# Modulation vectors by transposed loads and dot products, V in a tile of its own, two sets of gate and up weights

## The chip, the cores and the metric

One core of one Trainium2 chip runs the whole kernel. The metric is the device time of one execution in microseconds (us). Before the change the median of 10 runs is 1286.09 us (1285.23 to 1288.04).

## The reference

A transformer block on 2048 tokens of width 1024, in bfloat16, whose two layer norms are modulated by a conditioning vector c:

```python
mod = (_silu(c) @ w_mod).reshape(1, 6, 1, -1)      # c: 1 x 1024, w_mod: 1024 x 6144
sa, ca, ga, sb, cb, gb = (mod[:, i] for i in range(6))
h = layernorm(x) * (1 + ca) + sa
x = x + ga * attention(h)
h = layernorm(x) * (1 + cb) + sb
x = x + gb * ((silu(h @ w_gate) * (h @ w_up)) @ w_down)
```

The attention has 32 query heads of 128 columns over 4 cached key and value heads, of which the last 512 positions are used: q = h @ wq, scores scaled by 128 ** -0.5, softmax, times V, then the output projection wo (4096 x 1024). The inner width of the feed-forward part (FFN) is 3584. All weights are bfloat16.

## The kernel before

A guarded fast path (`fast_path`) does all the work; a general path follows only if a bound computed on the side says that the softmax without a maximum might overflow.

The tokens are cut into four chunks `cc` of 512. The attention is one sequence of 128 head units `k` (4 chunks x 32 heads). In unit `k` the program emits the scores of head `k` (`emit_s`, L1032: four matmuls of 512 columns, and two exponentials on ScalarE, L1034, which give `pT`), the q projection of head `k + 3` (`emit_q`, L1019: eight matmuls; VectorE casts the result to `qT`, L916), the side tasks planned for that unit, and the product with V of head `k - 1` (`emit_o`, L1064: 4 token tiles x 4 value blocks `j`, with `pT` as weights and V as the moving operand). A column of ones beside V makes the same matmul give the softmax denominator; VectorE takes its reciprocal (L1046) and scales (L1051) when three token tiles have filled a PSUM bank. The token tiles of one head come in groups of three that run on over heads.

Side tasks are written down by hand with `at(k, ...)`: the output projection (`emit_wo`, L1096, eight matmuls a unit from unit 13 on, evicted by VectorE at L1102, L1104 or L1108 to L1111), layer-norm statistics and transposes for later chunks, loads of x and wo, and a sum of squares of wq (`bound_wq`, L955) from unit 32 on. The modulation vectors are among them. Shift and scale of the first norm (`sa`, `ca1`) are made at the start (`mod_cols`, L753). The other four come in two rounds of 16 units: `load_rows` loads w_mod in natural layout, 1 MB at a time; `mod_rows` (L779) multiplies it with `sil32` (silu(c) repeated over 32 columns), four matmuls side by side in column groups of 32; VectorE evicts (L784, L788) into a block called `row`; the result goes to DRAM (`row_d`), and is read back as a broadcast row (`load_gate`, for the gates `ga_bc` and `gb_bc`) or as columns (`load_cols`, for `cb1` and `sb`; `cb1` gets one added on VectorE, L802).

After unit 127 comes the FFN, chunk by chunk: seven groups `fg` of four inner tiles, each with four weight tiles of 512 KB (two of w_gate, two of w_up; `load_gu`, `emit_gu` L1168), then the down projection (`emit_down`, L1188) in two halves `dh` of 512 output columns, each with seven w_down tiles (`load_wd`). The last output-projection units run between the first FFN groups.

In SBUF, blocks of some 4 KB per partition are shared by pools: `blkA` (8 buffers: `pT`, accumulators, the FFN's products), `blkB` (7: kT, V, wq, then gate and up weights) and `blkC` (13: `oq`, `oT`, `wo`, `row`, then w_down). w_mod pieces and normalized chunks share the pool `hT` (4). PSUM has a pool `mm` of 4 banks for q, o, output projection and down projection, and a pool `s` of 2 double banks for scores and the FFN.

While the attention is emitted, all loads and DMA transposes go through SP's queue (`fetch`, L664; `xpose_o`, L1081; `ln_xpose`, L848) in program order, and the vector instructions marked with `pin` keep their order. In the FFN the framework's scheduler orders the loads. A buffer that is still in use holds up the load that is to fill it, and with it the queue. Outputs leave by ScalarE's queue.

Of the kernel before, what the change touches and what calls it, by code (L numbers as in the profile page):

```python
# [9 lines left out]
ALU = mybir.AluOpType  # L10
AX = mybir.AxisListType
BF16 = mybir.dt.bfloat16
# [576 lines left out]
def fast_path(ctx, tc, flag, A_x, A_k_cache, A_v_cache, A_wq, A_wo, B_x, B_w_gate, B_w_up,  # L589
# [3 lines left out]
    nc = tc.nc  # L593
# [37 lines left out]
    hpool = ctx.enter_context(tc.tile_pool(name="hT", bufs=4))  # L631
    pa_ = ctx.enter_context(tc.tile_pool(name="blkA", bufs=8))
    pb_ = ctx.enter_context(tc.tile_pool(name="blkB", bufs=7))
    pc_ = ctx.enter_context(tc.tile_pool(name="blkC", bufs=13))
    wk = ctx.enter_context(tc.tile_pool(name="work", bufs=2))
    sm = ctx.enter_context(tc.tile_pool(name="small", bufs=4))
    psp = ctx.enter_context(tc.tile_pool(name="psum", bufs=4, space=bass.MemoryType.PSUM))
# [5 lines left out]
    def blkB(name, shape, dt=BF16):  # L643
        return pb_.tile(shape, dt, name=name, tag="B")
# [57 lines left out]
    for kv in range(Hkv):  # L702
        pin(nc.sync.dma_start_transpose(
            out=kT[:, kv, :], in_=A_k_cache[0, kv, k0:k0 + W, :]), "dma")
    VW = Dh + 4
    v_sb = blkB("v_sb", [P, Hkv, WT, VW])
    for kv in range(Hkv):
        load(v_sb[:, kv, :, 0:Dh], v_v[:, kv])
    nc.gpsimd.memset(v_sb[:, :, :, Dh:VW], 1.0)
    load_wq(0, 1)  # L710


# [45 lines left out]

    sil32 = const.tile([P, DT, 32], BF16, name="sil32")
    for dt in range(DT):
        nc.vector.tensor_scalar(out=sil32[:, dt, :], in0=ones_bf[:, 0:32],
                                scalar1=siluc[:, dt:dt + 1], scalar2=None, op0=ALU.mult)
    wm_rows = []
    row_part = []
    row_d = {}

    def load_rows(vec, part):
        t = hpool.tile([P, 4, D], BF16, name="wmr", tag="hT")  # L770
        load(t, wm_v[:, 4 * part:4 * part + 4, vec * D:(vec + 1) * D])
        wm_rows.append(t)

    def mod_rows(n, part):
        ps = mm("row_ps")
        tiles = [wm_rows.pop(0) for _ in range(2)]
        for k in range(4):
            for i in range(4):
                nc.tensor.matmul(ps[32 * i:32 * i + 32, :], lhsT=sil32[:, 4 * part + k, :],  # L779
                                 rhs=tiles[i // 2][:, k, (i % 2) * 512:(i % 2 + 1) * 512],  # L780
                                 start=(k == 0), stop=(k == 3))
        if part == 0:
            r = blkC("row", [P, TCW], FP32)
            nc.vector.tensor_copy(out=r, in_=ps)  # L784
            row_part.append(r)
        else:
            r = row_part.pop()
            nc.vector.tensor_tensor(out=r, in0=ps, in1=r, op=ALU.add)  # L788
            d = dp.tile([4, TCW], FP32, name="row_d", tag="row_d", bufs=2)
            fetch(out=d, in_=r[0:P:32, :])  # L790
            row_d[n] = d

    def load_gate(n, k, dst):
        fetch(out=dst.rearrange("p (a b) -> p a b", a=2),
                          in_=row_d[n][k:k + 2, :].partition_broadcast(P))

    def load_cols(n, k, dst, add_one):
        src = row_d[n][k:k + 2, :].rearrange("a (b p) -> p (a b)", p=P)
        with nc.allow_non_contiguous_dma(reason="1024 values to columns"):
            fetch(out=dst, in_=src)  # L800
        if add_one:
            nc.vector.tensor_scalar(out=dst, in0=dst, scalar1=1.0, scalar2=None, op0=ALU.add)  # L802

    tasks = {}

# [248 lines left out]
    def emit_o(g):  # L1054
        cc, h = divmod(g, H)
        kv = h // rep
        if h % 4 == 0:
            oq[(cc, h // 4)] = blkC("oq", [P, QT, 4, Dh])
        for t in range(QT):
            if o_slot["n"] == 0:  # L1060
                o_slot["ps"] = mm("o_ps", (P, SLOTS, Dh + 1))
            s_ = o_slot["n"]
            for j in range(WT):
                nc.tensor.matmul(o_slot["ps"][:, s_, :], lhsT=pT[g][:, j, t * P:(t + 1) * P],  # L1064
                                 rhs=v_sb[:, kv, j, 0:Dh + 1], start=(j == 0),
                                 stop=(j == WT - 1))
            runs = o_slot["runs"]
            if runs and runs[-1][0] == g:
                runs[-1][2] = t + 1
            else:  # L1070
                runs.append([g, t, t + 1, s_])
            o_slot["n"] = s_ + 1
            if o_slot["n"] == SLOTS or (t == QT - 1 and h % HQ == HQ - 1):
                close_bank()
        del pT[g]
# [35 lines left out]
            nc.vector.tensor_tensor(out=x1, in0=f, in1=x1, op=ALU.add)  # L1111


    for n, vecs in enumerate(((2, 4), (5, 3))):
        for part in range(2):
            k = 16 * n + 8 * part
            at(k, load_rows, vecs[0], part)
            at(k + 2, load_rows, vecs[1], part)
            at(k + 5, mod_rows, n, part)
        at(16 * n + 15, load_gate, n, 0, gb_bc if n else ga_bc)  # L1120
        at(16 * n + 16, load_cols, n, 2, sb if n else cb1, n == 0)
    for tt in range(QT, S // P):
        cc, t = divmod(tt, QT)
        at(max((cc - 1) * H - 16, 0) + 2 + 2 * t, load_x, tt)
# [26 lines left out]
    gu_w = {}  # L1151
    wd_tiles = {}

    def load_gu(cc, fg):
        for nm, v in (("wg", wg_v), ("wu", wu_v)):
            for i in range(2):
                t = blkB(nm, [P, 4, 512])
                load(t, v[:, 4 * i:4 * i + 4, fg * 512:(fg + 1) * 512])
                gu_w[(cc, fg, nm, i)] = t

# [113 lines left out]
```

## Time and profile before

| | |
|---|---|
| median of 10 runs | 1286.09 us |
| lowest, highest | 1285.23, 1288.04 us |
| the profiled execution: its time | 1285.31 us |
| its span, first to last instruction | 1283.5 us |
| TensorE's granted clock, mean | 0.998 |
| TensorE busy (matmuls) | 1263.0 us, 98% |
| VectorE busy | 578.1 us, 45% |
| ScalarE busy | 334.0 us, 26% |
| DMA | 204.20 MB, 159 GB/s on average |
| q, scores, o matmuls | 1024 and 512 of 512 columns, 2048 of 129 columns |
| row matmuls for four modulation vectors | 64 of 512 columns, 32 weight columns each |

The profile is of one execution. The page gives busy time, instruction groups by line, and waits; the trace behind it can be asked for a stretch of time, a line or a tile. Matmuls are pipelined, so the recorded length of one is longer than the distance to the next: distances between starts tell what a matmul costs. A few per cent of matmul records are missing. Units of the attention last 3.5 us up to unit 12 (without an output projection) and 5.24 us from unit 14 on.

### The profile page before, as it was taken

What the parts mean: (1) busy time and instruction counts of PE and PEld (TensorE: products, weight loads), DVE (VectorE), ACT (ScalarE), POOL (GpSimd) and SP (SyncE); (2) the same over time, 40 slices, a digit from 0 to 9 for tenths busy, and PEclk for the clock granted to TensorE, in tenths of its full rate; (3) what the DMA queues carried; (4) which work ended last, traced back from release to release, by engine and by line L of the source; (5) the groups of instructions that cost most, each with busy time, mean ns of one, the idle gap of its engine ahead of it and who ended that gap; (6) DMA issues with size and microseconds to landing.
All of it is one profiled execution on the core that took longest, in us unless ns stands there. A gap on an engine that the chain in (4) does not pass through costs nothing.

```text
span 1283.5 us, 18000 instructions
## 1 busy us (share of the span) xinstructions
PE 1263.0 (98%) x7461; PEld 644.1 (50%) x7601; DVE 578.1 (45%) x1271; ACT 334.0 (26%) x433; POOL 1.3 (0%) x8
## 2 busy tenths in 40 slices
PE   8999999999999999999999999999999999999998
PEld 4555555555555555555554444444444444444444
DVE  4464567866577755576663642221212121221122
ACT  3543334343333433333341111011100111011100
POOL 0000000000000000000000000000000000000000
PEclk9999999999999999999999999999999999999999
DMA  9878466456345654445568384454536445454401
GB/s 290 275 203 220 162 149 172 135 144 202 96 123 156 148 140 148 116 148 131 132 171 272 124 251 151 140 188 144 179 104 219 142 163 165 135 193 133 146 19 34
DMA packets 280107, 204.20 MB, mean 159 GB/s; under 512 B 113865, under 2 KB 273609, under 8 KB 280018
## 3 DMA queue, kind: packets, MB, share of 16 engines
q1 hardware_dynamic: 275106, 198.78, 52.3%
q10 hardware_dynamic: 4912, 4.20, 1.0%
q8 instruction: 61, 1.00, 0.3%
q14 instruction: 28, 0.23, 0.1%
HBM read 174.08 MB, written 4.21 MB: 139 GB/s over the span
## 4 chain that ended last, share of the span: by engine, by line
PE 96%; DMA 2%; DVE 1%; issue 1%; SPq 0%; ACT 0%; DVEq 0%
PE gu_ps L1168 29%; PE a_ps L1096 17%; PE q_ps L1019 17%; PE d_ps L1188 15%; PE o_ps L1064 9%; PE s_ps L1032 8%; DMA wm<-in_w_mod_dram 1%; PE q_ps L940 0%; DMA modT<-row_d 0%; DMA wu<-in_B_w_up_dram 0%; PE row_ps L779 0%; DMA hT<-xn 0%; SPq L664 0%; PE mod_ps L753 0%; DVE st L816 0%
## 5 line engine op out<-in xcount | busy, mean ns | idle before, releaser
L1034 ACT ACTIVATE pT<-s_ps 128x1024 bf16<-128x1024 f32 x256 | 248.6, 1020 | 343.8 <-PE s_ps L1032 229.6
L1096 PE MATMUL a_ps<-wo,oT 128*128 128x512 bf16 x986 | 239.9, 379 | 3.0 <-DVE acc L1102 1.0
L1019 PE MATMUL q_ps<-hT,wq 128*128 128x512 bf16 x999 | 236.7, 379 | 0.3 <-DVE modT L755 0.3
L1168 PE MATMUL gu_ps<-hT,wu 128*128 128x512 bf16 x875 | 209.9, 379 | 1.8 <-DMA wu<-in_B_w_up_dram 0.7
L1168 PE MATMUL gu_ps<-hT,wg 128*128 128x512 bf16 x879 | 210.0, 379 | 0.9
L1174 DVE TENSOR_TENSOR guT<-gu_ps,sg 128x512 bf16<-128x512 f32 x112 | 77.4, 691 | 283.7 <-ACT sg L1173 283.7
L1173 ACT ACTIVATE sg<-gu_ps 128x512 bf16<-128x512 f32 x112 | 66.9, 597 | 489.6 <-PE gu_ps L1168 426.9
L1188 PE MATMUL d_ps<-wd,guT 128*128 128x512 bf16 (+2 forms) x935 | 193.3, 366 | 0.9
L916 DVE CAST qT<-q_ps 128x512 bf16<-128x512 f32 x128 | 88.3, 691 | 177.2 <-PE q_ps L1019 176.7
L1096 PEld LDWEIGHTS <-oT 128*128 128x128 bf16 x1024 | 99.9, 98 | 122.3 <-issue 2.1
L1019 PEld LDWEIGHTS <-wq 128*128 128x128 bf16 x1000 | 97.8, 98 | 117.8 <-issue 0.3
L1064 PEld LDWEIGHTS <-pT 128*128 128x128 bf16 x2048 | 128.4, 97 | 30.6 <-issue 0.4
L1188 PEld LDWEIGHTS <-guT 128*128 128x128 bf16 x952 | 90.9, 98 | 103.0
L1168 PEld LDWEIGHTS <-wu 128*128 128x128 bf16 x896 | 87.6, 98 | 106.7 <-DMA wu<-in_B_w_up_dram 1.2
L1168 PEld LDWEIGHTS <-wg 128*128 128x128 bf16 x896 | 87.7, 98 | 105.5
L1064 PE MATMUL o_ps<-v_sb,pT 128*128 128x129 bf16 x2048 | 139.2, 219 | 0.0
L1032 PE MATMUL s_ps<-qT,kT 128*128 128x512 bf16 x467 | 128.9, 378 | 3.0 <-ACT pT L1034 0.6
L1051 DVE TENSOR_TENSOR oq<-o_ps,rl 128x256 bf16<-128x256 f32 (+2 forms) x256 | 101.3, 420 | 4.3
L1192 DVE TENSOR_TENSOR f<-d_ps,gb_bc 128x512 f32<-128x512 f32 (+2 forms) x34 | 22.5, 660 | 147.0 <-PE d_ps L1188 133.2
L1104 DVE TENSOR_TENSOR acc<-a_ps,acc 128x512 f32<-128x512 f32 x64 | 44.1, 689 | 40.8 <-PE a_ps L1096 40.8
L1032 PEld LDWEIGHTS <-kT 128*128 128x128 bf16 x512 | 44.7, 97 | 31.9 <-issue 1.3
L816 DVE BATCH_NORM_STATS2 st<-x 128x6 f32<-128x512 bf16 x64 | 41.3, 680 | 2.6 <-DMA x<-in_A_x_dram 2.4
(75 smaller groups left out, 307.6 us busy)
## 6 DMA issues: line engine op xcount, KB each, us to landing
wq<-in_A_wq_dram SPq DMA_DIRECT2D x64, 512.0 KB, 4.3
wo<-in_A_wo_dram SPq DMA_DIRECT2D x64, 512.0 KB, 5.4
wg<-in_B_w_gate_dram SPq DMA_DIRECT2D x56, 512.0 KB, 4.8
wu<-in_B_w_up_dram SPq DMA_DIRECT2D x56, 512.0 KB, 5.5
wd<-in_B_w_down_dram SPq DMA_DIRECT2D x56, 512.0 KB, 7.1
wmr<-in_w_mod_dram SPq DMA_DIRECT2D x8, 1024.0 KB, 8.7
x<-in_A_x_dram SPq DMA_DIRECT2D x16, 256.0 KB, 5.4
wm<-in_w_mod_dram SPq DMA_DIRECT2D x4, 1024.0 KB, 10.4
```

The source lines that it names most:

```text
L916: nc.vector.tensor_copy(out=t, in_=q_ps)
L1019: nc.tensor.matmul(q_ps, lhsT=wq_tiles[(cc, h // 4, dt // 4)][:, dt % 4, (h % 4) * P:(h % 4 + 1) * P], rhs=hT[("h1", cc)][:, dt, :], start ...
L1032: nc.tensor.matmul(s_ps[:, i, :], lhsT=kT[:, kv, j * P:(j + 1) * P], rhs=qT[g], start=True, stop=True)
L1034: nc.scalar.activation(out=p[:, 2 * jj:2 * jj + 2, :], in_=s_ps, func=ACT.Exp, scale=scale)
L1051: nc.vector.tensor_tensor(out=dst, in0=ps[:, s0:s0 + cnt, 0:Dh], in1=sc, op=ALU.mult)
L1064: nc.tensor.matmul(o_slot["ps"][:, s_, :], lhsT=pT[g][:, j, t * P:(t + 1) * P], rhs=v_sb[:, kv, j, 0:Dh + 1], start=(j == 0), stop=(j == W ...
L1096: nc.tensor.matmul(a_ps, lhsT=oT[(cc, 2 * q + i)][:, hh % 4, t * P:(t + 1) * P], rhs=wo_tiles[(cc, q, dh, i)][:, hh % 4, :], start=(hh == ...
L1104: nc.vector.tensor_tensor(out=acc[(cc, t)][:, dsl], in0=a_ps, in1=acc[(cc, t)][:, dsl], op=ALU.add)
L1168: nc.tensor.matmul(ps[:, n, :], lhsT=gu_w[(cc, fg, nm, dt // 4)][:, dt % 4, fi * P:(fi + 1) * P], rhs=hT[("h2", cc)][:, dt, :], start=(dt ...
L1173: nc.scalar.activation(out=g, in_=ps[:, 0, :], func=ACT.Silu)
L1174: nc.vector.tensor_tensor(out=guT[(cc, fg)][:, fi, :], in0=ps[:, 1, :], in1=g, op=ALU.mult)
L1188: nc.tensor.matmul(d_ps, lhsT=guT[(cc, f // 4)][:, f % 4, t * P:(t + 1) * P], rhs=wd_tiles[(cc, dh, f // 4)][:, f % 4, c0:c0 + w], start=( ...
```

## The change

Four things change together.

V moves out of `blkB` into a tile of its own, with 160 elements (320 bytes) per row instead of 132 (264 bytes), two ones columns instead of four, and 130 columns in the o matmul instead of 129. So `blkB` has six buffers for wq during the attention instead of five.

The four later modulation vectors are no longer made on TensorE. silu(c) goes to DRAM as a row and comes back broadcast over the partitions (`c_bc`). w_mod is loaded by DMA transposes, four of [1024 x 128] for each half vector, one half vector every four units from unit 1 to 29. In each of the units 4 to 35 VectorE does one dot product of 1024 elements per partition, which gives 128 values of a modulation vector as one column. `cb1` and `sb` are then in place (one is added to `cb1`); the two gates go to DRAM as columns and come back as broadcast rows. `sil32`, `row` and the row matmuls are gone.

`blkC` has 12 buffers instead of 13.

In the FFN the fourth tile of every second group (the second half of w_up) is loaded into the first 4096 bytes of V's tile, which by then is free. With the seven buffers of `blkB` that makes eight tiles, two full sets.

```diff
-    pc_ = ctx.enter_context(tc.tile_pool(name="blkC", bufs=13))
+    pc_ = ctx.enter_context(tc.tile_pool(name="blkC", bufs=12))
...
-    VW = Dh + 4
-    v_sb = blkB("v_sb", [P, Hkv, WT, VW])
+    VN = Dh + 2
+    v_sb = const.tile([P, Hkv, WT, Dh + 32], BF16, name="v_sb")
...
-    nc.gpsimd.memset(v_sb[:, :, :, Dh:VW], 1.0)
+    nc.gpsimd.memset(v_sb[:, :, :, Dh:VN], 1.0)
...
-    def load_rows(vec, part):
...
-    def mod_rows(n, part):
...
-    def load_cols(n, k, dst, add_one):
...
+    def spread_c():
+        fetch(out=c_d, in_=sil_r)
+        fetch(out=c_bc.rearrange("p (a b) -> p a b", a=DT), in_=c_d.partition_broadcast(P))
+
+    def load_wmT(vec, part):
+        t = hpool.tile([P, 4, D], BF16, name="wmT", tag="hT")
+        for i in range(4):
+            c0 = vec * D + (4 * part + i) * P
+            pin(nc.sync.dma_start_transpose(out=t[:, i, :], in_=w_mod[:, c0:c0 + P]), "dma")
+        wm_cols[(vec, part)] = t
+
+    def mod_dot(vec, j, dst):
+        t = wm_cols[(vec, j // 4)]
+        junk = wk.tile([P, D], BF16, name="junk", tag="junk", bufs=1)
+        pin(nc.vector.scalar_tensor_tensor(out=junk, in0=t[:, j % 4, :], scalar=1.0, in1=c_bc,
+                                           op0=ALU.mult, op1=ALU.mult,
+                                           accum_out=dst[:, j:j + 1]))
+
+    def add_one(dst):
+        pin(nc.vector.tensor_scalar(out=dst, in0=dst, scalar1=1.0, scalar2=None, op0=ALU.add))
+
+    def store_gate(n):
+        d = dp.tile([DT, P], FP32, name="col_d", tag="col_d", bufs=2)
+        with nc.allow_non_contiguous_dma(reason="columns to 1024 values"):
+            fetch(out=d.rearrange("a p -> p a"), in_=mod_col[:, n, :])
+        col_d[n] = d
+
+    def load_gate(n, dst):
+        fetch(out=dst.rearrange("p (a b) -> p a b", a=DT), in_=col_d[n].partition_broadcast(P))
...
-                o_slot["ps"] = mm("o_ps", (P, SLOTS, Dh + 1))
+                o_slot["ps"] = mm("o_ps", (P, SLOTS, VN))
...
-                                 rhs=v_sb[:, kv, j, 0:Dh + 1], start=(j == 0),
+                                 rhs=v_sb[:, kv, j, 0:VN], start=(j == 0),
...
-    for n, vecs in enumerate(((2, 4), (5, 3))):
+    at(0, spread_c)
+    for i, (vec, dst) in enumerate(((2, mod_col[:, 0, :]), (4, cb1), (3, sb),
+                                    (5, mod_col[:, 1, :]))):
         for part in range(2):
-            k = 16 * n + 8 * part
-            at(k, load_rows, vecs[0], part)
-            at(k + 2, load_rows, vecs[1], part)
-            at(k + 5, mod_rows, n, part)
-        at(16 * n + 15, load_gate, n, 0, gb_bc if n else ga_bc)
-        at(16 * n + 16, load_cols, n, 2, sb if n else cb1, n == 0)
+            k = 1 + 8 * i + 4 * part
+            at(k, load_wmT, vec, part)
+            for j in range(4):
+                at(k + 3 + j, mod_dot, vec, 4 * part + j, dst)
+        k = 1 + 8 * i + 10
+        if vec == 4:
+            at(k, add_one, cb1)
+        elif vec in (2, 5):
+            at(k + 1, store_gate, vec // 5)
+            at(k + 2, load_gate, vec // 5, gb_bc if vec == 5 else ga_bc)
...
+    v_flat = v_sb.rearrange("p a b c -> p (a b c)")
+    v_blk = v_flat[:, 0:2048].rearrange("p (a b) -> p a b", a=4)
...
-                t = blkB(nm, [P, 4, 512])
+                spare = (cc * NFG + fg) % 2 == 1 and nm == "wu" and i == 1
+                t = v_blk if spare else blkB(nm, [P, 4, 512])
```

More of the change, by code (lines that the diff above doesn't have):

```diff
@@ L756, in mod_cols @@
                                 scalar1=1.0 if add_one else 0.0, scalar2=None, op0=ALU.add)
[L761 to L767, printed above, removed]
-    def load_rows(vec, part):
-        t = hpool.tile([P, 4, D], BF16, name="wmr", tag="hT")
-        load(t, wm_v[:, 4 * part:4 * part + 4, vec * D:(vec + 1) * D])
-        wm_rows.append(t)
@@ L774, in mod_rows @@
-    def mod_rows(n, part):
[L775 to L791, printed above, removed]
@@ L793, in load_gate @@
-    def load_gate(n, k, dst):
-        fetch(out=dst.rearrange("p (a b) -> p a b", a=2),
-                          in_=row_d[n][k:k + 2, :].partition_broadcast(P))
-    def load_cols(n, k, dst, add_one):
[L798 to L802, printed above, removed]
+    c_d = dp.tile([DT, P], BF16, name="c_d", tag="c_d", bufs=1)
@@ new lines, in fast_path @@
+    c_bc = const.tile([P, D], BF16, name="c_bc")
+    mod_col = const.tile([P, 2, DT], FP32, name="mod_col")
+    wm_cols = {}
+    col_d = {}
+    def spread_c():
[7 more added lines that the diff above has]
+        wm_cols[(vec, part)] = t
```

## The prediction

> **What bounds the kernel now.** I read the page's first part, then the list of what TensorE waited for, then TensorE's instructions in order of time, and last the vector and DMA-issuing queues around the few places where TensorE pauses.
>
> ```profile
> PE 1263.0 (98%) x7461; PEld 644.1 (50%) x7601; DVE 578.1 (45%) x1271; ACT 334.0 (26%) x433; POOL 1.3 (0%) x8
> ```
>
> TensorE is the bound nearly everywhere, so only its own time and its pauses count. Its waits are few (columns: total us, times, longest):
>
> ```profile
> PE mod_ps L753 <- DMA wm<-in_w_mod_dram: 2.0, 2, 1.2
> PE a_ps L1096 <- DVE acc L1102: 1.0, 1, 1.0
> PE gu_ps L1168 <- DMA wu<-in_B_w_up_dram: 0.7, 1, 0.7
> ```
>
> The timeline of TensorE from 42 us on (start, length, instruction) shows the row matmuls between the q and o matmuls of one head:
>
> ```profile
> 43.45 1.89 PE L1019 MATMUL q_ps<-hT,wq 128*128 128x512 bf16 x8
> 45.27 1.05 PE L779 MATMUL row_ps<-wmr,sil 128*32 128x512 bf16 x16
> 46.25 1.10 PE L1064 MATMUL o_ps<-v_sb,pT 128*128 128x129 bf16 x16
> 47.19 1.02 PE L1032 MATMUL s_ps<-qT,kT 128*128 128x512 bf16 x3
> ```
>
> Starts are what matter, since lengths overlap. In dense stretches a 512-column matmul starts every 215.8 ns (eight in 1.726 us), so q ended at 43.45 + 1.73 = 45.17, yet o began at 46.25: the 16 row matmuls cost 1.08 us. The vector queue at 86 to 92 us shows the pause of L1096:
>
> ```profile
> 86.74 0.54 DVE L835 TENSOR_SCALAR xn<-x,mv 128x1024 bf16<-128x1024 bf16 x1
> 90.94 0.17 DVE L802 TENSOR_SCALAR modT<-modT 128x8 f32<-128x8 f32 x1 [3.66 <-DMA modT<-row_d]
> 91.02 0.69 DVE L816 BATCH_NORM_STATS2 st<-x 128x6 f32<-128x512 bf16 x1
> 91.62 0.68 DVE L1102 COPY acc<-a_ps 128x512 f32<-128x512 f32 x1
> ```
>
> The add-one on cb1 holds VectorE 3.66 us for a DMA; the accumulator copy behind it frees its PSUM bank late. Start to start, TensorE loses 1.18 us there. Near 754.5 us, a late half of w_up costs 0.87 us, also by starts. From 29 us to the last matmul I find no other pause of 30 ns or more besides the four row groups.
>
> **What the Trainium skill says.** "TensorE: Matmul & The Clock Gate", "Wait, 56ns, not 53.3ns?", spaces warm matmuls by N/2.4 ns + about 2.5: 215.8 for 512 agrees. For 129 it gives 56.25, but the o groups disagree: averaged over the trace by position, starts after value block j=0, 1, 2, 3 are 56.1, 59.9, 55.8, 59.4 ns apart, mean 57.8. "SBUF — State Buffer", "Specifications (TRN2)", names 16-byte lines with a penalty for crossings. V rows of 264 bytes start at 0 or 8 within such a line in turn, which fits the alternation; so would an odd column count. The change removes both. The opening table of the TensorE page makes VectorE's queue strictly first in, first out: L802 above agrees. "DMA: Bandwidth & Descriptors", "Latency and other measured facts", gives 261 GB/s for a transpose with a non-contiguous middle dimension; here the 256-byte packets of transposes take 17 ns each on 16 engines, 241 GB/s.
>
> **The change, part by part.** Sums are against the profiled execution: span 1283.45, its own time 1285.31, against a median of 1286.09.
>
> *Row matmuls.* Four groups disappear: 1.08 + 1.06 + 1.07 + 1.08 = 4.29 us saved on TensorE.
>
> *The column fetch.* cb1 no longer comes through a DMA that VectorE waits for: 1.18 us saved. Its add-one now follows a dot product on the same queue.
>
> *V.* 130 columns give 130/2.4 + 2.5 = 56.7 ns by the page; the even blocks' 55.83 plus 0.42 gives 56.25. I take 56.4. Saved: 2048 x (57.8 - 56.4) = 2.9 us. Bounds: 3.2 us if 56.25 holds; if neither alignment nor parity matters, a loss of 2048 x 0.42 = 0.9.
>
> *Gate and up buffers.* Eight tiles (seven of blkB and the first 4096 bytes of V) let a set load during the whole set before it. Only one TensorE wait is there to remove: 0.87; I count it whole (bounds 0 and 0.9). During attention the freed slot does nothing: wq has at most four tiles live at its loads.
>
> *blkC 13 to 12.* By allocation and last use I count at most four oT, six wo and two oq live, 12; row, the thirteenth, is gone. In the FFN dh=1 then has five w_down tiles ahead instead of six; the sixth starts when dh=0's last block (6.04 us) passes its first four matmuls and is used some 9 us later, against 7.1 us to landing. Without that cover each of the four switches from dh=0 to dh=1 would wait up to a landing, 7 us. I count 0.
>
> *Vector work.* 32 dot products of 1024 elements. The nearest row is L955, 1.216 us plus 0.083 for its accumulator read: 32 x 1.30 = 41.6 us, one per head in units 4 to 35. Removed: 8 scalings (1.2), four row evictions (2.8), and the wait. The rest of the queue is what it must fit beside. VectorE by stretch (heads 10-12, 13-17, 32-35, 36-44; columns: from and to, length, VectorE busy, its instructions, granted clock, DMA share, GB/s):
>
> ```profile
> 61.20:71.80 10.60, 6.47 (x19) 1.00 0.84 152
> 71.80:100.20 28.40, 16.98 (x41) 1.00 0.87 245
> 175.70:196.70 21.00, 14.63 (x34) 1.00 0.51 130
> 196.70:243.90 47.20, 38.16 (x85) 1.00 0.60 168
> ```
>
> The first becomes 6.47 + 3.9 = 10.4 of 10.6; the second 16.98 - 0.7 + 6.5 = 22.8 of 26.1; the third 14.6 + 5.2 = 19.8 of 21. The fourth runs at 81% today without a pause. Behind a dot product wait the qT cast, the acc copy and the bank evictions, and for those TensorE's four PSUM banks; L802 showed that 4.4 us of lateness cost 1.2, so some 3 us are covered. Heads 10-12 with their statistics build up about 2 us. I charge 1.5 us (bounds 0 and 10).
>
> *DMA queue.* Eight 1 MB loads (0.5 us of issue each) become 32 transposes of 256 KB; both move 8 MB. At 17 ns per 256-byte packet that is 1.09 us of all engines each, 34.8 in all, where 2 KB packets of 88 ns took 22.5. Issue time per transpose:
>
> ```profile
> L1081 SPq DMA_TRANSPOSE oT<-oq x128: 1188/1256/3296, 43.4 to 680.8; - x128
> L703 SPq DMA_TRANSPOSE kT<-in_A_k_cache_dram x4: 1266/1486/2937, 14.8 to 20.9; - x4
> ```
>
> (minimum/median/maximum ns.) At 1.25 that is 40 us of SP's queue, in fours at heads 1, 5, 9 and so on, ahead of each next wq load. Also c_bc must wait on SP until c_d has landed: the like pair gd_d, gd_row took 3 us in a quiet queue, and here two weight loads stand before it, so c_bc goes out near 31 us, four transposes fill 31.5 to 36.6, and the wq halves for head 8 go out at 36.7 and 38 instead of 26.5 and 30, wanted at 43.4 and 44.3, with 4.3 us to landing. Later, oT leaves SP at most 2 us late, and head 16's second wq half goes out about 64.7, wanted near 71.3. Margins of 1 to 2.5 us; I charge 0.9 (bounds 0 and 15). The gate stores (1024 four-byte pieces each) have a head before their reader; the before's fetch of such pieces landed in 5.1 us. Start-up isn't touched: VectorE's 1.2 us of scalings lie beside TensorE's wait for wm.
>
> *Sum.* Saved 4.29 + 1.18 + 2.9 + 0.87 = 9.2; new pauses 2.4; net -6.8. Profiled 1285.31 - 6.8 = 1278.5; a median stood 0.78 above it, so **1279.3 us**.
>
> **Rivals.**
> *VectorE becomes the bound.* Heads 10-13 and 32-35 have no room left, and if each of their eight dot products comes through to TensorE, 10.4 us are lost, net +1.2: 1287.3, no measurable change. For it: 98% in heads 10-12. Against it: 81% sustained costs nothing now. 13%.
> *Transposes hold up SP, and the change is slower.* w_mod's rows lie 12 KB apart, and no transpose here reads such a source. Twelve are issued before head 16's wq; each us over 1.25 delays that load 12 us, less 2.6 of margin. It decides where 12d - 2.6 outgrows about 7.7 (9.2 less VectorE's 1.5), at d = 0.86, 2.1 us apiece; at 2.5 us the pause is 12.4, net +4.7: 1290.8. For it: kT's first took 2.9[...], and engines are at 0.77 to 0.87 here. Against: wm reads 1 KB pieces of the same rows at the rate of contiguous wq. 15%.
> *V's padding and the buffers do nothing.* o stays at 57.8 and the w_up wait stays: 1279.3 + 2.9 + 0.9 = 1283.1, just at the bound. 10%, half of it no change.
>
> **How the numbers follow.** The forecast holds with 62%, from 1276.9 (no new pause) to 1282. About 0.2% (2.6 us) is what a measurement can tell from no change. Faster: 62 + 5 and 1 from a mild VectorE case, 68%; same: 5 + 11, 16%; slower: 15 and 1, 16%. From 1276.5 to 1288 leaves out 3% below and some 15% above.
>
> **What would show it.** Right: no L779 rows; o groups of 16 start to next start 0.90 us instead of 0.925; no DVE wait for modT; no w_up wait; 32 accumulating VectorE instructions of 1.2 us. Wrong: TensorE waits on qT, acc or pT at heads 10-17 or 32-40 (VectorE); TensorE waits on wq, or transposes of 2 us and more at 31 to 75 us (SP); VectorE waiting for wmT or c_bc; w_down waits after 800 us (blkC).

## The result, and the profile after

The changed kernel takes 1295.19 us in the median (1293.66 to 1300.01, 9 runs); the kernel before, beside it, 1286.21 (1284.76 to 1290.16, 30 runs). The ratio is 1.007, with a 95% interval of 1.006 to 1.008: slower by about 9 us, where 7 us faster was forecast. The profiled execution took 1294.26 us, with a span of 1292.5, against 1285.31 and 1283.5 before.

The page's first part, changed kernel: TensorE has 65 fewer instructions and is busy 2 us less, and yet the span is 9 us longer. The time is in pauses.

```profile
PE 1260.9 (98%) x7396; PEld 641.2 (50%) x7537; DVE 607.3 (47%) x1323; ACT 333.9 (26%) x433; POOL 1.2 (0%) x8
```

TensorE's waits in the changed kernel (us in total, times, longest us). The two waits that the change was to remove, for `acc` behind `modT` and for w_up, are gone. A wait for the q weights stands in their place, and a small one for `guT`, the FFN's product from VectorE, near the spot where w_up used to be late:

```profile
PE q_ps L1014 <- DMA wq<-in_A_wq_dram: 11.8, 3, 6.0
PE mod_ps L753 <- DMA wm<-in_w_mod_dram: 0.9, 1, 0.9
PE gu_ps L1174 <- DVE guT L1180: 0.7, 1, 0.7
```

TensorE's timeline near 44 us, where the row matmuls stood (start, length, instruction). The q matmuls are followed at once by o, and o to s_ps is 0.90 us, as forecast for groups of 16 (it was 0.94):

```profile
44.43 1.89 PE L1014 MATMUL q_ps<-hT,wq 128*128 128x512 bf16 x8
46.16 1.07 PE L1059 MATMUL o_ps<-v_sb,pT 128*128 128x130 bf16 x16
47.06 1.03 PE L1027 MATMUL s_ps<-qT,kT 128*128 128x512 bf16 x3
```

VectorE's timeline at 86 to 92 us: where it sat 3.66 us for `modT`, it now takes a dot product (1.22 us plus 0.08 for reading the accumulator), and the `acc` copy follows without a gap:

```profile
87.69 1.22 DVE L783 SCALAR_TENSOR_TENSOR junk<-wmT,c_bc 128x1024 bf16<-128x1024 bf16 x1
88.83 0.08 DVE L783 DVE_READ_ACCUMULATOR junk<-wmT,c_bc 128x1 f32 x1
88.83 0.55 DVE L830 TENSOR_SCALAR xn<-x,mv 128x1024 bf16<-128x1024 bf16 x1
89.28 0.69 DVE L1097 COPY acc<-a_ps 128x512 f32<-128x512 f32 x1
```

VectorE over the stretches of the forecast (from and to, length, VectorE busy, its instructions, granted clock, DMA share, GB/s). Later stretches hold slightly earlier heads than before, since up to 12 us have been lost by then. None is full; the first is at 90%:

```profile
61.20:71.80 10.60, 9.59 (x24) 1.00 1.13 209
71.80:100.20 28.40, 19.63 (x46) 1.00 0.78 146
196.70:243.90 47.20, 39.02 (x88) 1.00 0.83 150
```

So VectorE is not the cause of the loss. The transposes on SP's queue (minimum/median/maximum ns of issue), the old ones and the new ones:

```profile
L1076 SPq DMA_TRANSPOSE oT<-oq x128: 1188/1257/3102, 49.0 to 689.9; - x128
L777 SPq DMA_TRANSPOSE wmT<-in_w_mod_dram x32: 1165/1798/5202, 30.7 to 168.9; - x32
```

The new ones hold SP for 1.8 us in the median where I had put 1.25. Now SP's queue around the waits, in order (start, length in the queue, instruction):

```profile
64.64 0.58 SPq L664 DMA_DIRECT2D wo<-in_A_wo_dram  x1
65.32 0.45 SPq L664 DMA_DIRECT2D wq<-in_A_wq_dram  x1
65.87 5.48 SPq L1076 DMA_TRANSPOSE oT<-oq  x4
71.44 0.53 SPq L664 DMA_DIRECT2D wq<-in_A_wq_dram  x1
72.07 0.47 SPq L664 DMA_DIRECT2D col_d<-mod_col  x1
...
84.39 0.34 SPq L664 DMA_DIRECT2D ga_bc<-col_d  x1
84.78 9.60 SPq L777 DMA_TRANSPOSE wmT<-in_w_mod_dram  x4
...
95.29 0.44 SPq L664 DMA_DIRECT2D wq<-in_A_wq_dram  x1
...
103.14 0.53 SPq L664 DMA_DIRECT2D wq<-in_A_wq_dram  x1
```

The gate's store `col_d` goes out at 72.07; its reader `ga_bc`, which must wait for it to land, goes out at 84.39, 12.3 us later; the four transposes behind it take 9.6 us; then the first half of the next wq leaves at 95.29, when TensorE wants it, and the second at 103.14. TensorE answers (in brackets the idle time before, and what ended it):

```profile
75.56 1.04 PE L1014 MATMUL q_ps<-hT,wq 128*128 128x512 bf16 x4 [2.13 <-DMA wq<-in_A_wq_dram]
...
101.80 1.89 PE L1014 MATMUL q_ps<-hT,wq 128*128 128x512 bf16 x4 [6.04 <-DMA wq<-in_A_wq_dram]
107.28 1.89 PE L1014 MATMUL q_ps<-hT,wq 128*128 128x512 bf16 x4 [3.59 <-DMA wq<-in_A_wq_dram]
```

Start to start these pauses are 2.29, 6.20 and 4.00 us. From 100.9 us, near the end of the second, to 111.1 us TensorE has half its clock. A last view, slices of 4 us (columns as in VectorE's stretches), shows what the DMA engines did meanwhile:

```profile
74.00:78.00 4.00, 1.99 (x5) 1.00 0.69 124
78.00:82.00 4.00, 2.38 (x8) 1.00 0.28 19
82.00:86.00 4.00, 4.00 (x10) 1.00 0.39 24
86.00:90.00 4.00, 3.68 (x9) 1.00 1.05 225
```

While the store is under way they move 19 and 24 GB/s; from 86 us on it is 225 again. A low figure alone can also mean that nothing is asked for: the kernel before has such a slice, in which the engines are busy for 2% of the time, and the next is full:

```profile
74.00:78.00 4.00, 2.46 (x5) 1.00 0.02 6
78.00:82.00 4.00, 1.89 (x6) 1.00 1.01 286
```

Here transfers were waiting. The transpose `hT` sent at 72.63, right behind the store, landed after 13.2 us, the longest of all 28 (us from issue to landing, minimum/median/maximum):

```profile
DMA to landing us min/median/max: 3.1/3.3/13.2
```

The difference between the two profiled executions, followed by the start of each unit's first o matmul, is made up as follows:

| part | us |
|---|---|
| first unit starts later | +1.04 |
| row matmuls gone | -4.29 |
| pause behind `modT` gone | -1.18 |
| V, o matmuls closer together | -2.30 |
| three waits for wq | +12.49 |
| half clock behind them | +2.49 |
| small: unit 33, unit 40, score matmuls | +0.8 |
| sum; measured at the last down projection | 9.05; 9.02 |

The half clock is what is left at one place: between the first o of units 15 and 16 the difference grows by 12.69, of which 10.20 are the two pauses. The small part is 0.3 at unit 33, where an o matmul waits for VectorE's cast of `qT` (it starts at 196.96 us, the cast ends at 196.91), 0.2 at unit 40, a short wait for wq behind the second gate's store, and 0.26 by which the score matmuls give back part of V's gain: they start 215.8 ns apart where the kernel before has 215.2. Up to unit 15 the changed kernel is even (0.24 us ahead): all of the loss comes in one unit.

### The profile page after: what moved, and what is told of

It is laid out like the page before. It is cut to its first block, busy times and chain, and to the rows that moved or that the text cites. A ratio compares the mean times of both kernels' runs of the same rounds, so it can differ in the third digit from the quotient of the medians.

```text
span 1292.5 us, 17953 instructions
## 1 busy us (share of the span) xinstructions
PE 1260.9 (98%) x7396; PEld 641.2 (50%) x7537; DVE 607.3 (47%) x1323; ACT 333.9 (26%) x433; POOL 1.2 (0%) x8
## 4 chain that ended last, share of the span: by engine, by line
PE 93%; DMA 3%; DVE 2%; SPq 1%; issue 1%; ACT 0%; DVEq 0%
PE gu_ps L1174 28%; PE a_ps L1091 16%; PE q_ps L1014 16%; PE d_ps L1194 15%; PE o_ps L1059 9%; PE s_ps L1027 8%; DMA wm<-in_w_mod_dram 1%; DMA wq<-in_A_wq_dram 1%; DMA hT<-xn 1%; SPq L664 1%; SPq L1076 0%; PE q_ps L935 0%; DVE junk L950 0%; SPq L843 0%; DMA oT<-oq 0%
## 5 line engine op out<-in xcount | busy, mean ns | idle before, releaser
L1014 PE MATMUL q_ps<-hT,wq 128*128 128x512 bf16 x999 | 239.2, 381 | 12.1 <-DMA wq<-in_A_wq_dram 11.8
L1174 PE MATMUL gu_ps<-hT,wu 128*128 128x512 bf16 x659 | 162.0, 379 | 0.7
L1059 PE MATMUL o_ps<-v_sb,pT 128*128 128x130 bf16 x2048 | 137.3, 220 | 0.1
L1174 PEld LDWEIGHTS <-wu 128*128 128x128 bf16 x672 | 65.7, 98 | 79.3
L1174 PE MATMUL gu_ps<-hT,v_sb 128*128 128x512 bf16 x220 | 57.0, 379 | 0.2
```

The source lines that it names most:

```text
L1014: nc.tensor.matmul(q_ps, lhsT=wq_tiles[(cc, h // 4, dt // 4)][:, dt % 4, (h % 4) * P:(h % 4 + 1) * P], rhs=hT[("h1", cc)][:, dt, :], start ...
L1174: nc.tensor.matmul(ps[:, n, :], lhsT=gu_w[(cc, fg, nm, dt // 4)][:, dt % 4, fi * P:(fi + 1) * P], rhs=hT[("h2", cc)][:, dt, :], start=(dt ...
```

## The experiments

Theory: the gate's store of 1024 pieces of 4 bytes brings the DMA engines down for some 10 us, and what then stands on SP's queue ahead of wq (the broadcast load that waits for the store, and four transposes) makes wq late. Rivals: SP's idle wait alone; the transposes alone, slow because of their source; V or the buffers. All comparisons are with the kernel before on the same chip (1286.21 in the median beside the change, 1286.66 to 1287.12 beside the others).

| kernel | us | ratio to before, 95% interval |
|---|---|---|
| the change | 1295.19 | 1.006 to 1.008 |
| gate read back 8 units later | 1292.74 | 1.0035 to 1.0069 |
| gate stored in pieces of 32 bytes | 1283.53 | 0.9965 to 0.9984 |
| gate stored as rows of 512 bytes | 1284.54 | 0.9971 to 0.9986 |
| gate's store and reading back 2 units later | 1289.95 | 1.0011 to 1.0036 |
| all modulation tasks 2 units later | 1280.00 | 0.9933 to 0.9970 |
| the same with start-up scalings | 1281.22 | 0.9941 to 0.9968 |
| the same with rows of 512 bytes too | 1279.44 | 0.9929 to 0.9956 |
| modulation alone | 1298.07 | 1.0068 to 1.0099 |
| V and the buffers alone | 1284.30 | 0.9973 to 0.9986 |
| V alone (no spare tile) | 1287.37 | 0.9987 to 1.0004 |
| V and buffers, three idle 4-byte stores | 1287.77 | 0.9993 to 1.0011 |

### SP's idle wait alone

```diff
-            at(k + 2, load_gate, vec // 5, gb_bc if vec == 5 else ga_bc)
+            at(k + 10, load_gate, vec // 5, gb_bc if vec == 5 else ga_bc)
```

> Only the read-back of the two gates is planned eight units later (units 21 and 45 instead of 13 and 37). Theory 'gate wait' (the read-back holds SP's queue until the 4-byte store has landed, 8.46 us idle, and the wq loads for heads 19 and 20 behind it come late): the pauses at 95 to 107 us, 10.2 us and some 2.3 us at half clock, go; 1283 us, and the 2.3 us pause at 73 us stays. Theory 'transposes' (32 transposes at 1.8 us of SP's queue are what makes wq late): SP gets its idle 8.5 us back but stays late; at least 5 us of pauses remain at 90 to 110 us, about 1289 us.

1292.74: 2.5 us better, no more, and neither of the two expected times. The store still went out at 72.4, and the slices from 78 to 86 us still show 21 and 26 GB/s. The queue no longer waited for the store, but the transposes now stood in the starved stretch themselves, and one took 11.8 us to issue:

```profile
75.92 16.63 SPq L777 DMA_TRANSPOSE wmT<-in_w_mod_dram  x4
```

wq left at 93.68 instead of 95.29. So the idle wait as such explains little, and the stretch is as starved when SP does not idle; what is left to suspect is what the store does to the engines.

### Pieces of 32 bytes

```diff
-        d = dp.tile([DT, P], FP32, name="col_d", tag="col_d", bufs=2)
-        with nc.allow_non_contiguous_dma(reason="columns to 1024 values"):
-            fetch(out=d.rearrange("a p -> p a"), in_=mod_col[:, n, :])
+        d = dp.tile([P, DT], FP32, name="col_d", tag="col_d", bufs=2)
+        fetch(out=d, in_=mod_col[:, n, :])
```

> The gates are stored as 128 pieces of 32 bytes instead of 1024 of 4 bytes, and read back in that order, so the gates' values stand in the wrong columns and the output is not the reference's; all else as in the changed kernel. Theory 'gate wait': the store lands in about 3 us instead of 12.3, SP idles under 1 us before the read-back, w_o and w_mod loads at 76 to 86 us are not slow any more; 1283 us. Theory 'transposes': the wq loads stay late; about 1289 us.

1283.53. (The gates' values come back in another order.) The same 4 KB in 128 pieces of 32 bytes, at the same place of the queue, landed in 3.6 us, the `hT` transpose behind it in 4.3 instead of 13.2, and the stretch in question shows full traffic (the column of 0.65 and 1.00 is TensorE's clock):

```profile
78.00:82.00 4.00, 4.00 (x25) 0.65 1.12 288
82.00:86.00 4.00, 4.00 (x21) 1.00 0.95 154
```

wq left at 86.11, 9.2 us sooner, and of the three waits only the first is left:

```profile
PE q_ps L1013 <- DMA wq<-in_A_wq_dram: 3.1, 2, 2.8
```

The edit changes the number of pieces and their size together; no run here separates the two.

### Rows of 512 bytes

The gate is turned on TensorE by two matmuls of 128 columns (a high and a low bfloat16 part against the identity) and stored as 8 rows.

```diff
-            fetch(out=d.rearrange("a p -> p a"), in_=mod_col[:, n, :])
+        m = mod_col[:, n, :]
...
+        nc.tensor.matmul(g_ps, lhsT=hi, rhs=ident, start=True, stop=False)
+        nc.tensor.matmul(g_ps, lhsT=lo, rhs=ident, start=False, stop=True)
...
+        fetch(out=d, in_=g_sb)
```

> The changed kernel with its own plan of the modulation and without sil32, but the gate stored as 8 rows of 512 bytes as above. Theory (store and transposes together): without the 4-byte pieces the transposes before wq cost one delay at 72 to 77 us of 3 to 4 us, as with pieces of 32 bytes, and the waits of 6.2 and 4.0 us at 95 and 103 us are gone: 1283.5, at most 1285. Rival (the transposes ahead of wq are enough by themselves, and pieces of 32 bytes only happened to fall well): waits for wq of more than 8 us stay, 1292 to 1295.

1284.54, within the theory's bound. The broadcast load follows the store after 3.5 us (73.85 to 77.37), and one pause of 2.77 us at 74 us is left, with 3.4 us of half clock behind it. So the early transposes by themselves cost one pause of about 3 us; the waits of 6 and 4 us need the small pieces.

### Everything behind the wq halves

```diff
-            k = 1 + 8 * i + 4 * part
+            k = 3 + 8 * i + 4 * part
...
-        k = 1 + 8 * i + 10
+        k = 3 + 8 * i + 10
```

> All side tasks of the modulation are planned two units later (first transposes in unit 3 instead of 1), so that each four transposes stand behind both wq loads of their four units in SP's queue and not ahead of them; the gate store and its read-back move along, to units 14 and 15. Theory 'transposes': the wq waits of TensorE shrink from 12.5 us to under 3; about 1283 us. Theory 'gate wait': SP still idles 5 us or more before the read-back and the wq loads behind it are late; at least 6 us of TensorE waits for wq stay, 1288 us or more.

1280.00, faster than both kernels, 3 us better than the theory's figure, and 0.7 us from the time that was forecast for the change. The store is as slow as ever (13.6 us to landing in the version with start-up scalings, which has the same plan) and the engines starve (27 GB/s from 86 to 90 us), but now nobody waits, since the transposes follow a set's second wq half, and the next set's first half is out before the store:

```profile
67.25 0.53 SPq L664 DMA_DIRECT2D wq<-in_A_wq_dram  x1
67.83 5.96 SPq L777 DMA_TRANSPOSE wmT<-in_w_mod_dram  x4
...
76.43 0.45 SPq L664 DMA_DIRECT2D wq<-in_A_wq_dram  x1
76.98 0.45 SPq L664 DMA_DIRECT2D col_d<-mod_col  x1
...
90.29 0.52 SPq L664 DMA_DIRECT2D wq<-in_A_wq_dram  x1
90.91 0.45 SPq L664 DMA_DIRECT2D ga_bc<-col_d  x1
```

This moves two things at once, the transposes and the store. The store alone, two units later:

```diff
-            at(k + 1, store_gate, vec // 5)
-            at(k + 2, load_gate, vec // 5, gb_bc if vec == 5 else ga_bc)
+            at(k + 3, store_gate, vec // 5)
+            at(k + 4, load_gate, vec // 5, gb_bc if vec == 5 else ga_bc)
```

> The changed kernel with only the gate's store and its broadcast load planned two units later; the transposes stay where the change has them, ahead of the wq halves. It parts what the kernel with the later modulation tasks (1280.0) moved together. Theory: the store does its harm by the place it has, ahead of a group of transposes and a wq half. With the store behind them, the group at 76 us runs at 6 to 8 us and the first wq half leaves at about 85 instead of 95, so the wait of 6.2 us at 95 goes; the starved stretch falls on the oT transposes and the second half, and a wait of 0 to 4 us at 100 us may stay, beside the one of 2 to 3 us at 73: 1281 to 1287. Rival (transposes ahead of wq are the larger part, wherever the store stands): the waits for wq stay over 8 us in all, 1290 or more.

1289.95 (1285.04 to 1293.18, 9 runs), which is nearer to the rival than to the theory: the waits for wq come to 8.4 us, over the 8 that it names, and the time is 0.05 us short of its 1290. The theory's places were right: the transposes at 76 us took 7.0 us, the first half left at 83.73, the wait at 95 us went. Its sizes were not: the second half left only at 95.35, in the starved stretch (34 GB/s from 94 to 98 us), and TensorE lost 4.73 us at 100 and, in two pauses, 4.16 at 73. Moving the store gains 5.2 of the 15.2 us; the rest needs the transposes moved too. So the store did not do its harm by its place alone: with the transposes ahead of wq, it harms at either place, and without small pieces the same transposes cost one pause.

### The store by itself

Three such stores that nobody reads, added to the kernel with V and the buffers alone, whose modulation is that of before and has no transposes of w_mod:

```diff
+    for n, k in enumerate((12, 36, 60)):
+        at(k, store_col, n)        # 1024 pieces of 4 bytes, from a constant
```

> The modulation of the kernel before, with V's own tile and the spare weight tile (the kernel that measured 1284.3), and three stores added that nobody reads: 1024 pieces of 4 bytes from 128 partitions, like the gate's, at units 12, 36 and 60; no transposes of w_mod. Theory: the pieces by themselves bring the engines down. Then each store takes 6 to 12 us to land, a slice of 4 us behind it shows less than 60 GB/s, and since no transposes hold up the queue behind it TensorE loses at most 1 us per store: 1284 to 1287. Rival: store and transposes starve each other only together. Then each store lands within 4 us, the traffic behind it stays over 100 GB/s, and the time is 1284.3 within 0.5 us.

1287.77, 3.5 us over the 1284.30 without the stores: 0.8 us more than the theory allowed, and far from the rival. The first store went out at 65.82. The wo loads between 60 and 100 us, without the stores and then with them (us from issue to landing, minimum/median/maximum; the traces show the landing of three and of two of the four). The two sent at 70 and 77 us, shown in both, took 3.9 and 3.7 us without the stores and 11.1 and 6.6 with them:

```profile
DMA to landing us min/median/max: 3.6/3.9/6.7
```

```profile
DMA to landing us min/median/max: 6.6/8.8/11.1
```

and the slices behind it, the first wo load being under way:

```profile
70.00:74.00 4.00, 4.00 (x32) 1.00 0.93 95
74.00:78.00 4.00, 4.00 (x34) 1.00 0.42 33
```

TensorE's pause at 91 us behind `modT` grew from 1.15 to 3.52 us, with 6.8 us of half clock behind it, which cost 2.8. The other two stores cost TensorE nothing. Small pieces starve the other traffic without any help from the transposes of w_mod; what that costs depends on which load is due.

### The parts

> The modulation part of the change alone: V stays at 129 columns in rows of 264 bytes in its block, seven blocks B, thirteen blocks C. Theory: the parts add up. V with the buffers alone measured 1284.3, the change 1295.2, so this one takes 1286.2 + 10.9 = 1297, with the same waits for wq at 73, 95 and 103 us (2, 6 and 4 us, within 3 us each), and o matmuls of 57.8 ns on average. Rival: V's own tile or its queue place takes part in the delay of wq. Then the waits for wq are below 5 us together and the time is 1286 to 1291.

1298.07, as expected (1297): waits for wq of 3.2, 4.0 and 4.3 us at 73.6, 98.5 and 104.0 us, and one of 1.4 at 236 us behind the second gate's store. V's tile and its place in the queue have no part in the loss.

> The kernel before with the V part, the FFN's eight weight tiles and 12 blkC buffers, but with the modulation on TensorE as before. Both theories: the o matmuls start 56.67 ns apart, 2.3 us saved; the row groups and the modT pause stay; no wait for wq. 1284.0 us. If instead the slowdown comes from V, the buffers or blkC, this run is slower than 1288.

1284.30. The o matmuls start 56.67 ns apart after every j, the four row groups and the pause behind `modT` (1.15 us) are still there, and instead of w_up TensorE waits 0.65 us for `guT`. Without the spare tile:

```diff
-                spare = (cc * NFG + fg) % 2 == 1 and nm == "wu" and i == 1
-                t = v_blk if spare else blkB(nm, [P, 4, 512])
+                t = blkB(nm, [P, 4, 512])
```

> As the kernel that measured 1284.3 (modulation of the kernel before, V's own tile), but the weight pool alone serves gate and up: no spare tile in V's place. Theory: the spare tile is worth nothing, since the pause that it takes away at 754 us (0.87 us, waiting for w_up) is replaced by one of 0.5 to 1.1 us for VectorE's guT. Then a pause of 0.9 us or less on w_up or on guT is there and the time is 1284.3 within 0.6 us. Rival (the forecast's): it is worth 0.87 us, and the time is 1285.2.

1287.37, which fits neither figure: 3 us more, where 0 or 0.9 was expected. Of that the profile shows 1.8 at w_up (a pause of 2.47 us at 754.75, against 0.65), 0.8 at `modT` and 0.9 in the start-up, and the last two have nothing to do with the tile. The pause for w_up has no fixed size: 0.87 and 1.22 us in two executions of the kernel before, 1.49 with the modulation alone. So neither that the spare tile is worth nothing nor that it is worth 0.87 us is shown.

### What makes o slower: the row length or the odd count

V's rows of 264 bytes with 130 columns, and rows of 320 bytes with 129:

```diff
-    v_sb = const.tile([P, Hkv, WT, Dh + 32], BF16, name="v_sb")
+    v_sb = const.tile([P, Hkv, WT, Dh + 4], BF16, name="v_sb")
```

> The changed kernel with V's rows of 264 bytes, as before, and 130 moving columns. Theory: the alternation of 55.8 and 59.6 ns between even and odd j comes from the odd column count 129 and goes at 130 columns; all four j then stand at 56.67. Rival: it comes from rows of 264 bytes that start at a multiple of 16 or not; then even and odd j still differ by some 3.7 ns at 130 columns (56.3 and 60.0). The time is that of the changed kernel, 1295, within 1 us in the first case, and 2.3 us longer in the second.

```diff
-                                 rhs=v_sb[:, kv, j, 0:VN], start=(j == 0),
+                                 rhs=v_sb[:, kv, j, 0:Dh + 1], start=(j == 0),
```

> The changed kernel with V's rows of 320 bytes and 129 moving columns. Theory (odd count): even and odd j still differ, 55.8 and 59.6 ns, mean 57.8, and the time is 2.3 us over the changed kernel's. Rival (start of the rows): all j alike at 129/2.4 + 2.5 = 56.25 ns, 0.4 ns below 130 columns, and the time is 0.9 us below the changed kernel's.

The theory fell. The starts in the traces, averaged over the groups of 16, alternate with rows of 264 bytes at 130 columns just as at 129 (56.0, 59.8, 55.8, 59.3 ns after j = 0, 1, 2, 3); with rows of 320 bytes they stand at 56.67 at 129 columns too, not at the rival's 56.25. The padding is the whole gain, and the second column of ones neither costs nor brings anything. The times, 1296.35 and 1294.80, are too close to the changed kernel's to add to this.

### Why the transposes hold SP

> The changed kernel, but the transposes read blocks of 1024 x 128 that lie in one piece in the K cache in place of w_mod's columns, whose rows stand 12 KB apart; the modulation is therefore not the reference's. Theory: each transpose's issue on SP (1.8 us in the median, up to 5.2, where the forecast had 1.25) is time in which the queue is held back by source rows far apart. Then the issue median falls to 1.25 to 1.35, the groups of four ahead of wq shrink from 6 to 10 us to about 5, and the waits for wq from 11.8 to 5 to 9 us. Rival: it is held back by what the engines are busy with then, the store of 4-byte pieces first. Then the median stays at 1.6 to 1.8, single ones over 4 us remain, and the waits for wq stay at 10 to 12.5 us.

The issue stayed at 1.59 us in the median and 5.9 at most, and the waits for wq at 11.2 us, as the rival says (a second execution of the changed kernel has 1.65 and 5.3). Rows 12 KB apart are not the reason, or little of it:

```profile
L777 SPq DMA_TRANSPOSE wmT<-in_A_k_cache_dram x32: 1165/1592/5873, 31.4 to 169.5; - x32
```

In the kernels that put them behind the wq halves, the same transposes take 1.30 us in the median. The time depends on where they stand in the queue; by what exactly, no run here separates.

### The start-up

> The modulation tasks planned two units later, so that the transposes stand behind the wq halves, and the eight scalings of sil32 at start-up put back, although nothing reads their result. Theory: those scalings, dropped by the change, moved TensorE's half-clock stretch of 3.4 us from 14.7 us to 22.4 us, on to q matmuls, and that is the 1.04 us by which the first o matmul came later. Then the stretch is back at about 14.7, the first o starts at 30.2 to 30.6 instead of 31.6, and the time is 1279.0 (1 us below the 1280.0 without them). Rival: the later start has another cause (the two new transfers of c_d and c_bc, or the wq halves behind them). Then the first o stays at 31.3 to 31.6 and the time at 1280.0.

> The kernel before, unchanged, looked at once more, for the start-up alone. If the place of TensorE's half-clock stretch of 3.4 us (at 14.7 us in the first look) differs from one execution to the next, the first o matmul starts at 30.3 or at 31.3 to 31.7; if the kernel fixes it, the stretch stands at 14.7 again, and the first o at 30.3 within 0.2.

> The changed kernel, unchanged, looked at once more. If the three waits for wq and the starved stretch belong to the kernel, they stand again at 73, 95 and 103 us within 3 us each, with 10 to 13 us in all and less than 40 GB/s in two slices of 4 us behind the gate's store. For the start-up: half clock at 22.4 and the first o at 31.3 again if the kernel fixes it; otherwise either of the two places.

The scalings did not bring the start back: half clock stood at 22 us and the first o at 31.63, and the time was 1281.22. But the first o came at 30.40 in the kernel with rows of 512 bytes, which has the same start-up, at 31.46 in a kernel with the old modulation, and at 31.30, 30.90 and 30.28 in three executions with the changed kernel's program (the last with the other source). The kernel before gave 30.27 and 30.16. So the 1.04 us lie in where the half-clock stretch falls (from 14 to 18 us, beside the first norm's transposes, or at 21 to 26, on twelve q matmuls), and one program does not fix it: the execution with 30.28 has no such stretch at all, and the kernel with V's narrow rows and 130 columns has one at 16 and one at 23, and starts at 32.24. Over all profiled executions the first o stands at 31.48 in the median of 13 with the new start-up, and at 30.59 in the median of 5 with the old; that the change makes the later place likelier is possible and not shown. The second execution of the changed kernel shows the other findings again: pauses at 72.9, 97.4 and 101.7 us, 3.1, 3.4 and 4.5 us, and 18 and 28 GB/s from 78 to 86 us; a fourth pause of 1.2 us at 233 us follows the second gate's store.

### Both repairs together

The later tasks, the scalings, and the gate's rows of 512 bytes:

> As the kernel with the later tasks and the scalings, and the gate is turned into 8 rows of 512 bytes on TensorE (two small matmuls against the identity, high and low part) before it is stored, so no piece of 4 bytes is written. Theory: it is the 4-byte pieces that bring the DMA engines down to some 20 GB/s for 8 to 10 us. Then the store lands within 4 us, no slice of 4 us between 70 and 100 us shows less than 60 GB/s, and the time is that of the same kernel with the 4-byte store within 1 us, because there the starved stretch delayed nobody: 1278.5 to 1280. Rival: the engines starve because of the transposes behind the store, and the stretch of 20 GB/s stays. Second rival: TensorE waits for the last dot product before its two small matmuls, 1 to 3 us for each gate: 1281 to 1284.

1279.44, the fastest version, 0.58% below the kernel before; the one with the later tasks alone has an interval that overlaps. No slice of 4 us from 70 to 110 us is below 106 GB/s. TensorE's two small matmuls cost 0.57 us for each gate, by starts, and no wait for the last dot product is in the list.

## Why the prediction was wrong

**The DMA queue** is the step that failed: it was charged 0.9 us and cost 12.5. Its first wq loads left when forecast, 36.7 and 38 (36.73 and 37.90), but by luck: c_bc left 0.8 us early (30.23), and the four transposes took 6.0 us instead of 5.1. Three things in it did not hold.

First, "The gate stores (1024 four-byte pieces each) have a head before their reader; the before's fetch of such pieces landed in 5.1 us." I priced a store by a load of the same pieces. The store took 12.3 us, and I charged it only to its reader; the larger effect is on everyone else, with 19 to 24 GB/s left for all traffic. With pieces of 32 bytes or rows of 512 the loss turns into a gain, 1283.5 and 1284.5.

Second, 1.25 us for each transpose. The second and third group of four took 8.72 and 8.75 us, 2.2 apiece, before any store. Thus "head 16's second wq half goes out about 64.7" became 71.44, and TensorE paused 2.29 us at 73 us. That is the second rival's mechanism at its place. The mean of the twelve, 1.95 us, is just under the 2.1 at which it was to decide, and its price was too high there. The rule of 12 us per us over 1.25 gives about 12 x 0.7 - 2.6 = 5.9 us for the 23.5 us that the twelve took (15 were forecast); 2.3 came. The measured time lies beyond that rival's 1290.8 because of the store.

Third, I followed the queue to head 16's wq and no further, and charged 0.9 us. The waits of 6.2 and 4.0 us fall on the set after that one. The upper bound of 15 us was large enough for the 12.5 that came, but the stated range was not.

**Half clock** was not in the sum at all: 2.5 us behind the pauses. The Trainium skill, "TensorE: Matmul & The Clock Gate", "Part 1: The HAM clock gate (the "warmup" mystery)", puts the clock at half after an idle window of about 3.4 us; the pauses of 6.2 and 4.0 us with 10.2 us of half clock agree. As a threshold the figure does not hold here: 3.4 us of half clock also followed pauses of 2.44 us (V's narrow rows), 2.63 (129 columns) and 3.16 (modulation alone), though none followed 2.29 us in the changed kernel or 2.47 without the spare tile. A rival that forecasts a pause of some 2.4 us or more should add it.

**VectorE**: charged 1.5, cost 0.3. The 32 dot products took 1.215 + 0.083 us each in the median, as taken from the nearest row. The list of waits has none of TensorE on qT, acc or pT at heads 10 to 17 or 32 to 40, but by starts TensorE lost 0.3 us for `qT` at unit 33, one of the places that the first rival names; the kernel with later tasks, which has the same dot products, loses it too. At that size the rival is refuted.

**Row matmuls and the column fetch**: 4.29 and 1.18 us, right; all of it came.

**V**: 2.30 us instead of 2.9, and 0.26 of it is given back by the score matmuls. 56.4 ns was a mean of two guesses; the estimate of 56.67 from the Trainium skill's formula for 130 columns ("TensorE: Matmul & The Clock Gate", "Wait, 56ns, not 53.3ns?") is what was measured. The estimate of 56.25 for 129 columns was not: 56.67.

**Gate and up buffers**: counted as 0.87; in this pair of profiles 0, since the wait for w_up (0.87) was replaced by one for `guT` (0.86). The kernels without the spare tile lost 0.9 to 2.5 us there, those with it 0.5 to 2.3 for `guT`; no run fixes what is gained.

**blkC 13 to 12**: 0, right; no wait of the down projection appears. **Start-up**: "isn't touched", yet 1.0 us later in this profile, by the place of a half-clock stretch that differs from one execution to the next.

**A reading**: a 256-byte packet takes 18 ns in the median in the trace and one of 2 KB 84, not 17 and 88 (228 GB/s, not 241); nothing in the sum rests on it.

Put together, against the profiled executions: forecast -6.8, measured +8.95. The waits for wq account for 11.6 of the 15.8 us between them (12.5 for 0.9), the half clock for 2.5, V and the buffers for 1.5, the start for 1.0; VectorE's charge of 1.5 goes the other way, and the other 0.8 is that of unit 33, unit 40 and the score matmuls. With the tasks two units later and nothing else changed, the kernel took 1280.00: the forecast's net gain came to within 1 us, in part because errors cancel: V and the buffers brought some 1.5 us less, and of the 2.4 charged for pauses little was needed. The place in the queue, with the small pieces, undid the gain.

## What to carry to other kernels

Look at the pieces of a store, and charge it to all traffic, not only to its reader: 1024 pieces of 4 bytes cost a transpose behind them some 9 us here (13.2 against 4.3), the same 4 KB in 128 pieces nothing that could be seen. What it costs the bound engine depends on what is due: TensorE's waits behind the first gate's store came to 10 us in the changed kernel, those behind the second's, in all executions, to 1.4 at most. When work moves on to a DMA-issuing queue, follow that queue until the next two loads that the bound engine needs, and put the new work behind them: the same instructions two units later were worth 15 us. Add a half-clock stretch to any forecast pause of TensorE of some 2.4 us or more.

## What the runs showed of the hardware that was not expected

- The first store of 1024 pieces of 4 bytes, from 128 partitions, landed in 10.4 to 13.6 us in the eight executions whose traces show its landing, and two slices of 4 us behind it moved 12 to 95 GB/s. A load of 1024 pieces of 4 bytes landed in 5.1 us.
- An o matmul of 129 or 130 columns starts 56.67 ns after the one before when V's rows are 320 bytes, and some 56 and 59.6 ns in turn when they are 264 bytes, whatever the parity of the count.
- The same DMA transpose of 256 KB held its issuing queue for between 1.17 and 11.8 us, and the median went from 1.80 to 1.30 with the place in the queue, but only to 1.59 with a source in one piece (1.65 in a second execution with the old source).
- Half the clock came after pauses of TensorE of 2.44 us and more, but not after every one.
